# A chunked linear attention and two SwiGLU layers: decay tables turned earlier, state copies and normalising moved to ScalarE, and the last check split

## The chip, the cores and the metric

The kernel runs on one core of a Trainium2 chip. The metric is the time of one execution on the device in microseconds (us), the slowest core's, which here is the only one. Several executions are timed, and their median counts.

## The reference

```python
for t in range(768):                                    # 4 batches, 8 heads, head size 48, all f32
    cur = einsum('bhd,bhe->bhde', u * k[t], v[t])
    y[t] = einsum('bhd,bhde->bhe', r[t], state + cur)
    state = w * state + einsum('bhd,bhe->bhde', k[t], v[t])
x = y as (3072 tokens, 384)
x = (silu(x @ w_gate) * (x @ w_val)) @ w_out            # 384 -> 1536 -> 384
x = x / sqrt(mean(x * x) + 1e-6) * rms_g                # over the 384 of a token
out = (silu(x @ w_gate2) * (x @ w_val2)) @ w_out2
```

## The kernel before

**The attention** is cut into 32 units: 4 batches, 2 halves of the sequence, 4 pairs of heads. A unit scales its keys and queries by tables of powers of the decay `w` (`G` and `F`), computes the products inside a chunk on TensorE (PE), and carries a 128x48 state over the chunks. Batch 0 does this in f32 with chunks of 128; batches 1 to 3 split every operand into two f16 parts and use chunks of 64. `states` (L478 and L644) runs down the chunks on VectorE (DVE), one scalar_tensor_tensor each (`st <- st * w + pd`). A first half ends with a copy of its last state to `carry`, a second half begins with a copy of `carry` (L486, L491, L649, L657); a first half of batches 1 to 3 begins with a copy of the first product out of PSUM (L651).

**The tables** start from the 96 decays. Two DMAs each bring `w` and `u` as 8 rows (`wu_raw`), `turn_tables` (L230) transposes them on PE into PSUM, L235 copies them, and `setup_tables` (L267 to L291) and `setup_g` (L295) compute the powers on DVE in a chain of small instructions. While the loads run, PE multiplies zeros (`warm`, L321): `WARM = (28, 7)` says 28 such matmuls, then 7 before the second unit's output. The keys of each unit arrive in another layout and are transposed on DVE (L383); L391 on DVE and L394 on GpSimd (POOL) scale them, and the first product of the attention is L463.

**The layers** take the 3072 tokens in 8 blocks of 384, and 1536 hidden columns in 12 steps of 128. A step computes a gate and a value product on PE (L820), silu on ScalarE (ACT, L934), two multiplications on DVE (L942, L944), an f16 high part on ACT (L948), its remainder on POOL (L952), and three f16 matmuls per group of 128 tokens into `po` (L830), of which there are three (g = 0, 1, 2). The blocks of both layers are interleaved: (0,0), (0,1), (0,2), (1,0), (0,3), (1,1) and so on, (1,7) last. The weights of both layers come as raw words and are decoded on DVE (L785, L787, L789, L810) and ACT (L769, L774, L806) during the first third of the run.

At the end of a block `evacuate` (L832) scales `po` into `xo`: groups 0 and 2 on DVE, group 1 on ACT. `squares` (L846) sums the squares of `xo` on ACT; after layer 0 `inverse_rms` (L852) computes `ri` on POOL, `normalize` (L866) multiplies the three groups by it on DVE, `turn_x2` (L871) transposes them on DVE, and `store1` and `load_x2` send them over DRAM to layer 1. After layer 1 `store2` writes `out`. `check_range` (L960) then tests all the sums gathered on the way (squares, weight sums, decays in `wok`), adds them up with one PE matmul into `bad`, and every engine reads `bad` and branches to a general path when it isn't 0.

**The order** on every queue is made by a small list scheduler, `Plan` (L71). Each job has an engine, a cost, the jobs it comes after, and hints (`soon`); its rank is the longest path to the end. The job that can start first is taken, among several the one of the highest rank. Each engine then runs its own jobs strictly in that order.

## Time and profile before

| | us |
|---|---|
| median of 3 runs | 1048.23 |
| lowest and highest | 1045.59, 1048.25 |
| the profiled execution, its own time | 1051.98 |
| its span in the profile | 1050.3 |
| busy in it: PE, DVE, ACT, POOL | 978.8, 609.4, 518.7, 456.9 |
| mean granted clock of TensorE | 0.968 |

The times of instructions are those of the profiled execution, counted from the start of its span; 1.7 us of its time lie around the span. Busy shares are means over stages that differ much, so the stages are read apart. The granted clock is in parts of 2.4 GHz. L numbers are lines of the kernel before.

### The profile page before, as it was taken

The numbers are of one execution on the slowest core, as the hardware profiler recorded it, in microseconds if no ns is written. First come the engines' busy times: TensorE is split into PE (matmuls) and PEld (weight loads), VectorE is DVE, ScalarE is ACT, GpSimd is POOL, SyncE is SP. The second block draws the span as 40 slices with busy tenths as digits, with TensorE's granted clock in tenths as the row PEclk, the third lists the DMA queues.
The fourth block names the chain that finished last, engine by engine and source line by source line (L and its number), as shares of the span: only waits on it lengthen the run. The fifth ranks groups of instructions, "written<-read, shape, count | busy, mean of one in ns | idle before, by whom it ended". The sixth has DMA issues, their size and how long they took to land.

```text
span 1050.3 us, 20693 instructions
## 1 busy us (share of the span) xinstructions
PE 978.8 (93%) x8061; PEld 604.7 (58%) x8062; DVE 609.4 (58%) x1120; ACT 518.7 (49%) x1217; POOL 456.9 (43%) x502
## 2 busy tenths in 40 slices
PE   7778798897889999999999999999999999999995
PEld 4645554554555566656666666666666666666663
DVE  6999999999888754546354744645352412231111
ACT  1965566767685743536344643455343523242322
POOL 6257376545455444553355444553444223332221
PEclk8898899998999999999999999999999999999998
DMA  7997155449655421213113321222010100200000
GB/s 181 222 224 190 27 132 150 113 74 183 142 161 70 103 71 27 49 40 92 40 41 63 80 53 37 30 61 69 7 18 8 54 1 1 53 23 1 23 1 27
DMA packets 152699, 77.13 MB, mean 73 GB/s; under 512 B 115472, under 2 KB 141200, under 8 KB 152592
## 3 DMA queue, kind: packets, MB, share of 16 engines
q1 hardware_dynamic: 152208, 75.13, 31.6%
q8 instruction: 65, 1.06, 0.5%
q0 software_dynamic: 384, 0.59, 0.3%
q14 instruction: 42, 0.34, 0.1%
HBM read 66.23 MB, written 9.45 MB: 72 GB/s over the span
## 4 chain that ended last, share of the span: by engine, by line
PE 65%; DVE 13%; DMA 11%; SPq 5%; issue 3%; ACT 2%; POOL 1%; DVEq 0%; ACTq 0%; POOLq 0%
PE pg L820 20%; PE pv L820 20%; PE po L830 20%; DMA raw<-in_moe_w_out_dram 5%; DMA raw<-in_moe_w_gate_dram 3%; DVE fi L787 2%; PE py L611 2%; DVE w L810 2%; SPq L364 2%; DVE fi L789 1%; DMA xs_d<-tt 1%; DVE fi L785 1%; PE pa L622 1%; PE pd L622 1%; DVE st L654 1%
## 5 line engine op out<-in xcount | busy, mean ns | idle before, releaser
L820 PEld LDWEIGHTS <-w 128*128 128x128 f16 x3456 | 337.8, 99 | 246.8 <-issue 35.6
L952 POOL TENSOR_TENSOR hl<-sl,hh 128x384 f16<-128x384 f32 x192 | 186.3, 971 | 432.8 <-ACT hh L948 402.4
L830 PE MATMUL po<-w,hh 128*128 128x384 f16 x1152 | 281.7, 327 | 0.5 <-DVE xo L844 0.5
L948 ACT ACTIVATE hh<-sl 128x384 f16<-128x384 f32 x192 | 100.0, 521 | 342.3 <-DVE sl L942 193.9
L830 PE MATMUL po<-w,hl 128*128 128x384 f16 x576 | 187.9, 326 | 7.2 <-POOL hl L952 7.2
L820 PE MATMUL pg<-xh,w 128*128 128x384 f16 x576 | 164.2, 341 | 15.1 <-DVE sl L944 14.6
L820 PE MATMUL pv<-x2v,w 128*128 128x384 f16 x864 | 157.6, 328 | 2.5 <-ACT sl L934 2.5
L942 DVE SCALAR_TENSOR_TENSOR sl<-sl,pv 128x384 f32<-128x384 f32 x96 | 52.9, 551 | 183.6 <-PE pv L820 175.0
L820 PE MATMUL pv<-xh,w 128*128 128x384 f16 x576 | 158.2, 330 | 0.0
L820 PE MATMUL pg<-x2g,w 128*128 128x384 f16 x864 | 156.1, 326 | 2.1 <-DVE sl L942 1.7
L830 PEld LDWEIGHTS <-hh 128*128 128x128 f16 x1152 | 111.8, 98 | 74.0 <-issue 1.5
L944 DVE TENSOR_TENSOR sl<-sl,pv 128x384 f32<-128x384 f32 x96 | 52.4, 547 | 102.3 <-PE pv L820 102.1
L934 ACT ACTIVATE sl<-pg 128x384 f32<-128x384 f32 x192 | 92.8, 484 | 32.7 <-PE pg L820 30.4
L820 PE MATMUL pg<-xl,w 128*128 128x384 f16 x288 | 98.4, 342 | 0.0
L820 PE MATMUL pv<-xl,w 128*128 128x384 f16 x288 | 95.1, 330 | 0.0
L830 PEld LDWEIGHTS <-hl 128*128 128x128 f16 x576 | 56.4, 98 | 47.8 <-POOL hl L952 11.0
L787 DVE SCALAR_TENSOR_TENSOR fi<-raw,fi 128x384 int32<-128x384 int32 (+1 forms) x48 | 43.6, 915 | 1.1
L810 DVE SCALAR_TENSOR_TENSOR w<-fi,w 128x384 f16<-128x384 f32 (+1 forms) x48 | 42.6, 902 | 0.8 <-ACT w L806 0.6
L654 DVE SCALAR_TENSOR_TENSOR st<-st,p,pd 128x48 f32<-128x48 f32 x120 | 31.8, 265 | 19.3 <-PE pd L622 15.1
L789 DVE SCALAR_TENSOR_TENSOR fi<-raw,fi 128x384 int32<-128x384 int32 (+1 forms) x48 | 40.0, 848 | 0.7
L569 POOL TENSOR_TENSOR ap<-af,ap 128x384 f16<-128x384 f32 x24 | 25.1, 1044 | 33.9 <-ACT ap L566 33.9
L551 DVE STREAM_TRANSPOSE kf<-kts 128x384 f32<-128x384 f32 x24 | 20.8, 865 | 32.4 <-POOL kp L569 32.3
(190 smaller groups left out, 1257.0 us busy)
## 6 DMA issues: line engine op xcount, KB each, us to landing
...
```

The source lines that it names most:

```text
L569: eng.tensor_sub(t[:, 1], x, t[:, 0])
L654: nc.vector.scalar_tensor_tensor(out=st[:, c + 1], in0=st[:, c], scalar=self.w64(), in1=self.pd[:, c], op0=ALU.mult, op1=ALU.add)
L787: vec.scalar_tensor_tensor(out=fis[q], in0=high, scalar=-0x40000000, in1=fis[q], op0=ALU.bitwise_and, op1=ALU.bitwise_or)
L789: vec.scalar_tensor_tensor(out=fis[q], in0=low, scalar=29, in1=fis[q], op0=ALU.logical_shift_right, op1=ALU.bitwise_or)
L810: nc.vector.scalar_tensor_tensor(out=lo, in0=fis.pop(q).bitcast(F32), scalar=2.0**WS, in1=hi, op0=ALU.mult, op1=ALU.subtract)
L820: nc.tensor.matmul(pt, a[:, kt, :], x[:, kt, :], start=i == 0, stop=i == last)
L830: nc.tensor.matmul(po[g], a[:, sl], x, start=f == 0 and i == 0, stop=f == NF - 1 and i == 2)
L934: nc.scalar.activation(out=sl, in_=job[t]["g"], func=AF.Silu, scale=2.0 ** -(WS + (X2S if J[0] else X1S)))
L942: nc.vector.scalar_tensor_tensor(out=sl, in0=sl, scalar=2.0 ** (H2S - WS - V2S), in1=job[t]["v"], op0=ALU.mult, op1=ALU.mult)
L944: nc.vector.tensor_mul(sl, sl, job[t]["v"])
L948: nc.scalar.activation(out=job[t]["h"][0], in_=job[t]["sl"], func=AF.Copy)
L952: nc.gpsimd.tensor_sub(hl, job[t]["sl"], hh)
```

## The change

The 28 warm matmuls become 9 and 14, with `turn` between them, and it no longer waits for the whole of them. The last step of `states` writes straight to `carry`, and the copies that begin a half go from DVE to ACT. `normalize` goes from DVE to ACT. In layer 0 group 0 is evacuated on ACT as well as group 1. In the last block all three groups are evacuated on DVE, and its squares are read out of PSUM by ACT with the same scale; its last remainder `hl` is computed on DVE instead of POOL. The range check without the last block's sums runs before that block's end; the rest of it is a test of 128x3 values and four small matmuls. `wok` is computed after batch 0 rather than with the tables. The costs in the plan of the jobs concerned change with them, so the planner makes a new order.

```diff
 TOK_LO, MAG_MEAN, GAIN_LO = 2.5e-8 ** 2, 1.02, 0.01
+FINITE = 3.0e38
...
-WARM = (28, 7)
+WARM = (9, 14, 7)
...
             else:
-                nc.vector.tensor_copy(st[:, 0], carry[hp])
+                nc.scalar.activation(out=st[:, 0], in_=carry[hp], func=AF.Copy)
             for c in range(self.nd):
+                to = carry[hp] if c == NC - 1 else st[:, c + 1]
                 nc.vector.scalar_tensor_tensor(
-                    out=st[:, c + 1], in0=st[:, c], scalar=w128(hp), in1=self.pd[c], op0=ALU.mult, op1=ALU.add)
-            if self.half == 0:
-                nc.vector.tensor_copy(carry[hp], st[:, NC])
+                    out=to, in0=st[:, c], scalar=w128(hp), in1=self.pd[c], op0=ALU.mult, op1=ALU.add)
...
             if self.half:
-                nc.vector.tensor_copy(st[:, 0], late["carry"][self.hp])
+                nc.scalar.activation(out=st[:, 0], in_=late["carry"][self.hp], func=AF.Copy)
             else:
-                nc.vector.tensor_copy(st[:, 1], self.pd[:, 0])
+                nc.scalar.activation(out=st[:, 1], in_=self.pd[:, 0], func=AF.Copy)
                 c0 = 1
             for c in range(c0, self.nd):
+                to = late["carry"][self.hp] if c == N2 - 1 else st[:, c + 1]
                 nc.vector.scalar_tensor_tensor(
-                    out=st[:, c + 1], in0=st[:, c], scalar=self.w64(), in1=self.pd[:, c], op0=ALU.mult, op1=ALU.add)
-            if not self.half:
-                nc.vector.tensor_copy(late["carry"][self.hp], st[:, N2])
+                    out=to, in0=st[:, c], scalar=self.w64(), in1=self.pd[:, c], op0=ALU.mult, op1=ALU.add)
...
+    def on_act(layer, blk):
+
+        return () if (layer, blk) == (1, NBLK - 1) else (1,) if layer else (0, 1)
+
     def evacuate(layer, blk, g):
...
             scale = 2.0 ** -(X1S + 2 * WS)
-        if g == 1:
+        if g in on_act(layer, blk):
             nc.scalar.activation(out=xo, in_=po, func=AF.Copy, scale=scale)
...
             col = (layer * NBLK + blk) * NG + g
-            nc.scalar.activation(out=sq, in_=post["xo", layer, blk][:, g], func=AF.Square, accum_out=ssall[:, col : col + 1])
+            if (layer, blk) == (1, NBLK - 1):
+                nc.scalar.activation(out=sq, in_=acc[layer, blk][g], func=AF.Square, accum_out=ssall[:, col : col + 1],
+                                     scale=iratio[:, blk * NG + g : blk * NG + g + 1])
+            else:
+                nc.scalar.activation(out=sq, in_=post["xo", layer, blk][:, g], func=AF.Square, accum_out=ssall[:, col : col + 1])
...
         for g in range(NG):
-            nc.vector.tensor_scalar_mul(xo[:, g], xo[:, g], ri[:, 0, g : g + 1])
+            nc.scalar.activation(out=xo[:, g], in_=xo[:, g], func=AF.Copy, scale=ri[:, 0, g : g + 1])
...
         hh, hl = job[t]["h"]
-        nc.gpsimd.tensor_sub(hl, job[t]["sl"], hh)
+        (nc.vector if t == 2 * NT - 1 else nc.gpsimd).tensor_sub(hl, job[t]["sl"], hh)
...
         ns = 3 * (NBLK * HP - NU1)
-        ok = ev.tile([P, n + n // 2 + 3 * NW + ns + 1], F32, tag="sq", name="ok")
+        m = n - NG + n // 2 + 3 * NW + ns + 1
+        ok = ev.tile([P, m], F32, tag="sq", name="ok")
         g2 = ev.tile([P, KT], F32, tag="g2", name="g2")
...
         at = 0
-        for i, bound, op in ((ssall, 3.0e38, ALU.is_le), (ssall[:, : n // 2], TOK_LO * DM, ALU.is_ge),
+        for i, bound, op in ((ssall[:, : n - NG], FINITE, ALU.is_le), (ssall[:, : n // 2], TOK_LO * DM, ALU.is_ge),
                              (wsum[:, :NW], SUM_HI, ALU.is_le), (wsum[:, :NF], MAG_MEAN * 3 * DM, ALU.is_ge),
...
         nc.vector.tensor_reduce(out=m1[:, 1:2], in_=wok, axis=AX.X, op=ALU.min)
-        m2 = ev.tile([P, 1], F32, tag="m2", name="m2")
-        nc.vector.tensor_mul(m2, m1[:, 0:1], m1[:, 1:2])
+        post["m2"] = ev.tile([P, 1], F32, tag="m2", name="m2")
+        nc.vector.tensor_mul(post["m2"], m1[:, 0:1], m1[:, 1:2])
+
+    def check_last():
+
+        ok = ev.tile([P, NG], F32, tag="ok3", name="ok3")
+        nc.vector.tensor_scalar(out=ok, in0=ssall[:, -NG:], scalar1=FINITE, scalar2=None, op0=ALU.is_le)
         pc = ps.tile([P, 1], F32, tag="att0", name="pc")
-        nc.tensor.matmul(pc[0:1], m2, ones, start=True, stop=True)
+        for i in range(NG + 1):
+            nc.tensor.matmul(pc[0:1], ok[:, i - 1 : i] if i else post["m2"], ones, start=i == 0, stop=i == NG)
         bad = ev.tile([1, 1], I32, tag="bad", name="bad")
-        nc.vector.tensor_scalar(out=bad, in0=pc[0:1], scalar1=P - 0.5, scalar2=None, op0=ALU.is_lt)
+        nc.vector.tensor_scalar(out=bad, in0=pc[0:1], scalar1=(NG + 1) * P - 0.5, scalar2=None, op0=ALU.is_lt)
         return bad
...
     add("wu", "D", 1.9, [], load_tables)
-    add("turn", "T", 0.3, ["wu", "c0"], turn_tables)
+    add("turn", "T", 0.3, ["wu", ("warm", 0)], turn_tables)
     add("wraw", "V", 0.1, ["turn"], turned_tables)
...
     add("c1", "G", 1.2, [("v", HP - 1), "table"], setup_consts2)
-    for i, (m, after, soon) in enumerate(zip(WARM, (["c0"], [("d", 0)]), (("tb", 0), ("a", 1)))):
+    for i, (m, after, soon) in enumerate(zip(WARM, (["c0"], ["turn"], [("d", 0)]), ("turn", ("tb", 0), ("a", 1)))):
         add(("warm", i), "T", 0.22 * m + (3.2 if i == 0 else 0), after, lambda m=m: warm(m), soon=[soon])
...
         add(("G", hp), "V", 0.41, ["tables"], lambda hp=hp: setup_g(hp))
-    add("wok", "V", 0.4, ["tables"], decay_range)
+    add("wok", "V", 0.4, ["tables", ("xl", NU1 - 1)], decay_range)
...
         add(("sbd", n), "A", 0.61, [("st", n), "c1"] + prior("y", 2), lambda un=un: un.states2())
-        add(("y", n), "T", 1.95, [("below", n), ("sbd", n), ("f", n)] + prior("xl", back) * first + prior("y", 1) + [("warm", 1)] * (n == 1),
+        add(("y", n), "T", 1.95, [("below", n), ("sbd", n), ("f", n)] + prior("xl", back) * first + prior("y", 1) + [("warm", 2)] * (n == 1),
             lambda un=un, ytag=ytag: un.mm_y(ytag))
...
         add(("hh", t), "A", 0.41, [("m", t)] + prev("o", 2), lambda t=t: step_hh(t))
-        add(("hl", t), "G", 0.95, [("hh", t)], lambda t=t: step_hl(t))
+        add(("hl", t), "V" if t == 2 * NT - 1 else "G", 0.95, [("hh", t)], lambda t=t: step_hl(t))
         if f:
...
         for g in range(NG):
-            add(("e",) + J + (g,), "A" if g == 1 else "V", 0.41 if g == 1 else 0.47, [o] + before, lambda J=J, g=g: evacuate(*J, g))
+            add(("e",) + J + (g,), "A" if g in on_act(*J) else "V", 0.58, [o] + before, lambda J=J, g=g: evacuate(*J, g))
         es = [("e",) + J + (g,) for g in range(NG)]
-        add(("sq",) + J, "A", 1.4, es + [("sq",) + ORD[n_ - 1]] * (n_ > 0), lambda J=J: squares(*J))
+        add(("sq",) + J, "A", 2.1, ([o] if J == ORD[-1] else es) + [("sq",) + ORD[n_ - 1]] * (n_ > 0), lambda J=J: squares(*J))
         if layer == 0:
...
             add(("ri", blk), "G", 2.5, [("sq",) + J] + back("put") + back("sc"), lambda blk=blk: inverse_rms(blk))
-            add(("sc", blk), "V", 1.0, [("ri", blk)], lambda blk=blk: normalize(blk))
+            add(("sc", blk), "A", 1.6, [("ri", blk)], lambda blk=blk: normalize(blk))
             quot = [("vl2", b) for l, b in ORD[: n_ + 2] if l][-1:]
...
                     lambda blk=blk, g=g, n=n: store2(blk, g, g + n))
-    add("check", "V", 1.0, [("sq",) + J for J in ORD] + [("chk",) + q for q in seq] + ["wok", "attended"],
-        lambda: post.__setitem__("bad", check_range()))
+    add("check", "V", 3.0, [("sq",) + J for J in ORD[:-1]] + [("chk",) + q for q in seq] + ["wok", "attended", "rmsg"],
+        check_range)
+    add("bad", "V", 0.5, ["check", ("sq",) + ORD[-1]] + [("e",) + ORD[-1] + (g,) for g in range(NG)],
+        lambda: post.__setitem__("bad", check_last()))
...
         plan.run()
```

The first place is DVE at the start, from the zeroing of `uw` on. `first` holds the keys and queries of a unit, `wu` the turned decays. Before, the two transposes of the first unit stood ahead of the tables:

```order
L917 MEMSET uw 128x8
L383 STREAM_TRANSPOSE first_174<-first_174 128x12x32 [waits DMAHW6_49,DMAHW7_49,DMAHW5_49,DMAHW4_49]
L383 STREAM_TRANSPOSE first_174<-first_174 128x12x32 [waits DMAHW2_49,DMAHW3_49,DMAHW1_49,DMAHW0_49]
L235 COPY wu<-pw 128x8 [waits PE_49]
L270 TENSOR_SCALAR pw<-wu 128x4 [waits DVE_49]
L273 TENSOR_TENSOR pw<-pw 128x4 [waits DVE_49]
```

Now they stand behind nearly all of the tables (the second block begins with their last instruction but two):

```order
L292 TENSOR_SCALAR iE<-iE,zm 128x64 [waits DVE_49,Pool_49]
L384 STREAM_TRANSPOSE first_155<-first_155 128x12x32 [waits DMAHW2_49,DMAHW3_49,DMAHW1_49,DMAHW0_49]
L296 TENSOR_TENSOR G<-iE,ipw 128x128 [waits DVE_49]
L296 TENSOR_TENSOR F<-E,pw 128x128
L384 STREAM_TRANSPOSE first_155<-first_155 128x12x32 [waits DMAHW6_49,DMAHW7_49,DMAHW5_49,DMAHW4_49]
L392 TENSOR_TENSOR first_155<-first_155,G 128x384 [waits DVE_49]
L320 TENSOR_TENSOR uw<-wu,pw 64x4 x2
L384 STREAM_TRANSPOSE first_166<-first_166 128x12x32 [waits DMAHW6_49,DMAHW7_49,DMAHW5_49,DMAHW4_49]
```

The two L384 rows moved from ahead of the chain of small instructions into it.

The second place is ACT in the middle, where block (0,1) is normalised and the first second half of batch 1 starts. `w` is a decoded weight, `hh` and `sl` belong to a layer's step, `x2g` is a loaded block of layer 1, `sb` the scaled states that the unit's matmuls use. Before:

```order
L806 ACTIVATE w_2_2860<-fi_3049 128x384 [waits DVE_49]
L774 ACTIVATE mag,wsum<-mag,mlo 128x384 [waits Activation_49]
L806 ACTIVATE w_2_2860<-fi_3090 128x384 [waits DVE_49]
L934 ACTIVATE sl<-pg 128x384 [waits PE_49]
L906 ACTIVATE x2g<-xt,gains 128x384 [waits DMAHW6_49,DMAHW7_49,DMAHW5_49,DMAHW0_49]
L906 ACTIVATE x2g<-xt,gains 128x384 x2
L665 ACTIVATE sb<-st,p_100 64x6x48 [waits DVE_49]
L665 ACTIVATE sb<-st,p_100 64x6x48
```

Now three multiplications by `ri`, of which the first waits for POOL, and the copy of `carry` stand there, ahead of `hh` and `sl` of a step and of `sb`:

```order
L805 ACTIVATE w_2_2849<-fi_3006 128x384 [waits DVE_49]
L773 ACTIVATE mag,wsum<-mag,mlo 128x384 [waits Activation_49]
L805 ACTIVATE w_2_2849<-fi_3027 128x384 [waits DVE_49]
L876 ACTIVATE xo<-xo,ri 128x384 [waits Pool_49]
L876 ACTIVATE xo<-xo,ri 128x384 x2
L649 ACTIVATE st<-carry_1313 128x48
L955 ACTIVATE hh<-sl 128x384 [waits DVE_49]
L941 ACTIVATE sl<-pg 128x384 [waits PE_49]
L664 ACTIVATE sb<-st,p_100 64x6x48 [waits DVE_49,Activation_49]
L664 ACTIVATE sb<-st,p_100 64x6x48
```

Behind each of the waiting rows stand those of other chains, which start only after it.

The third place is the end of the program, on DVE first. Before, the last evacuation is followed by the whole check, which ends so:

```order
L975 TENSOR_SCALAR ok<-sqs 128x72
L975 TENSOR_SCALAR ok<-gs 128x1 [waits DVE_49]
L979 TENSOR_REDUCE m_13225<-ok 128x1 [waits DVE_49]
L980 TENSOR_REDUCE m_13225<-wok 128x1
L982 TENSOR_TENSOR m_13228<-m_13225 128x1 [waits DVE_49]
L986 TENSOR_SCALAR bad<-pc 1x1 [waits PE_49]
```

Now:

```order
L949 SCALAR_TENSOR_TENSOR sl<-sl,pv 128x384 [waits PE_49,Activation_49,Pool_49] x10
L959 TENSOR_TENSOR hl<-sl,hh 128x384 [waits Activation_49]
L847 TENSOR_SCALAR xo<-po_12804,iratio 128x384 [waits DMAHW6_49,PE_49]
L847 TENSOR_SCALAR xo<-po_12805,iratio 128x384 [waits Activation_49]
L847 TENSOR_SCALAR xo<-po_12806,iratio 128x384 [waits Activation_49]
L995 TENSOR_SCALAR ok_13209<-ssall 128x3
L1000 TENSOR_SCALAR bad<-pc 1x1 [waits PE_49]
```

The reductions moved ahead of the last block's end, `hl` and three evacuations stand where two did, and the second and third of these wait for ACT. On ACT the end is now:

```order
L955 ACTIVATE hh<-sl 128x384 [waits DVE_49,Pool_49]
L941 ACTIVATE sl<-pg 128x384 [waits PE_49]
L955 ACTIVATE hh<-sl 128x384 [waits DVE_49,Pool_49]
L854 ACTIVATE sq,ssall<-po_12804,iratio 128x384 [waits DVE_49]
L854 ACTIVATE sq,ssall<-po_12805,iratio 128x384 [waits PE_49,Activation_49]
L854 ACTIVATE sq,ssall<-po_12806,iratio 128x384 [waits PE_49,Activation_49]
```

The squares read `po` instead of `xo`; the first waits for DVE's evacuation of the same tile, the others for PE and for the square ahead of them.

## Rows read from the trace of the kernel before

**Rows 1.** Stretches: span, busy us of PE, PEld, DVE, ACT, POOL; clock, DMA share, GB/s.

```profile
30.00:130.00 100.00, 78.81 (x515) 52.93 (x516) 95.43 (x120) 67.58 (x117) 51.58 (x39) 0.88 0.69 163
130.00:330.00 200.00, 170.84 (x1587) 103.29 (x1587) 190.22 (x356) 142.47 (x386) 109.11 (x118) 0.94 0.59 133
...
400.00:1000.00 600.00, 599.06 (x4999) 368.75 (x4998) 251.46 (x485) 252.22 (x578) 238.20 (x268) 1.00 0.17 38
```

**Rows 2.** Waits of PE, 130 to 330 us: total us, times, longest us.

```profile
PE pg L820 <- DVE sl L944: 7.6, 5, 3.2
PE py L611 <- DVE sb L667: 7.5, 4, 4.1
...
PE pv L820 <- ACT sl L934: 2.5, 1, 2.5
...
PE py L611 <- ACT ap L566: 2.3, 2, 1.3
PE pg L820 <- DVE sl L942: 1.7, 1, 1.7
```

**Rows 3.** Timeline of the start: start us, us, engine, line, operation, count, [idle before].

```profile
4.78 0.15 PEld L325 LDWEIGHTS <-zeros 128*128 128x128 bf16 x1 [0.27 <-issue]
...
6.96 0.86 DVE L383 STREAM_TRANSPOSE first<-first 128x384 f32<-128x384 f32 x1 [5.35 <-DMA first<-in_k_dram]
...
9.24 0.87 DVE L383 STREAM_TRANSPOSE first<-first 128x384 f32<-128x384 f32 x1 [1.43 <-DMA first<-in_r_dram]
...
10.23 0.22 PE L232 MATMUL pw<-ident,wu_raw 8*128 8x8 f32 x1
10.49 0.17 DVE L235 COPY wu<-pw 128x8 f32<-128x8 f32 x1 [0.38 <-PE pw L232]
...
14.84 1.24 POOL L394 TENSOR_TENSOR first<-first,F 128x384 f32<-128x384 f32 x1 [4.83 <-DVE F L295]
```

**Rows 4.** Groups of lines on DVE, 20 to 130 us.

```profile
L486 DVE COPY st<-carry 128x48 f32<-128x48 f32 x4 | 2.2, 546 | 0.0
...
L491 DVE COPY carry<-st 128x48 f32<-128x48 f32 x4 | 1.4, 354 | 0.1
```

**Rows 5.** The same on DVE, 130 to 330 us.

```profile
L869 DVE TENSOR_SCALAR xo<-xo,ri 128x384 f32<-128x384 f32 x9 | 4.4, 544 | 0.0
...
L844 DVE TENSOR_SCALAR xo<-po 128x384 f32<-128x384 f32 x6 | 3.0, 548 | 0.0
...
L657 DVE COPY carry<-st 128x48 f32<-128x48 f32 x4 | 2.3, 569 | 0.1
...
L651 DVE COPY st<-pd 128x48 f32<-128x48 f32 x4 | 0.8, 194 | 0.0
L649 DVE COPY st<-carry 128x48 f32<-128x48 f32 x3 | 0.5, 175 | 0.0
```

**Rows 6.** Groups of lines on ACT over the whole span.

```profile
L496 ACT ACTIVATE sbd<-st,p 64x144 f32<-64x144 f32 x16 | 6.5, 408 | 4.1 <-DVE st L488 4.0
L842 ACT ACTIVATE xo<-po,iratio 128x384 f32<-128x384 f32 x8 | 4.6, 580 | 5.3 <-PE po L830 5.3
```

**Rows 7.** Timeline of a block's end in the PE-bound part.

```profile
432.36 1.11 DVE L869 TENSOR_SCALAR xo<-xo,ri 128x384 f32<-128x384 f32 x3 [3.15 <-POOL ri L859]
...
434.02 0.52 ACT L948 ACTIVATE hh<-sl 128x384 f16<-128x384 f32 x1 [3.52 <-DVE sl L942]
```

**Rows 8.** Timeline of the end of the program.

```profile
1037.47 0.91 POOL L952 TENSOR_TENSOR hl<-sl,hh 128x384 f16<-128x384 f32 x1 [3.47 <-ACT hh L948]
...
1038.81 0.62 DVE L844 TENSOR_SCALAR xo<-po,iratio 128x384 f32<-128x384 f32 x1 [2.03 <-PE po L830]
...
1040.41 0.52 ACT L850 ACTIVATE sq<-xo 128x384 f32<-128x384 f32 x1
...
1041.06 0.52 ACT L850 ACTIVATE sq<-xo 128x384 f32<-128x384 f32 x1
...
1043.51 0.15 DVE L986 TENSOR_SCALAR bad<-pc 1x1 int32<-1x1 f32 x1 [0.28 <-PE pc L984]
```

## The prediction

> **What bounds the kernel now.** I read the table of stretches first [rows 1]. From 400 to 1000 us PE is busy for 599.06 of 600 us at a granted clock of 1.00: there PE is the bound, and work taken off another engine gives nothing. From 30 to 130 us DVE is busy 95.43 of 100, and from 130 to 330 us 190.22 of 200, while PE has 170.84 of 200: PE sits idle for 29.2 us in the second of these stretches, and DVE hardly at all. So the first third is paced mostly by DVE, which decodes the weights there. The change can gain in three places only: the time before DVE is full (the start), the first third, and the end, where one chain runs alone.
>
> Next the waits of PE in the second stretch [rows 2]. Three of them end on a DVE instruction, 7.6 + 7.5 + 1.7 = 16.8 us, and two on an ACT instruction, 2.5 + 2.3 = 4.8 us. Of PE's 29.2 idle us, 0.58 are thus DVE's and 0.16 ACT's; the rest is mainly POOL's. The reader should see that taking 1 us from DVE need not give 1 us, and that ACT, busy 142.47 of 200 [rows 1], isn't free either.
>
> Then the timelines of the start [rows 3] and the end [rows 8], where single instructions count.
>
> **The change part by part.** The sum is made against the profiled execution's 1051.98 us, 3.75 above the median of 1048.23; I carry the difference to the median.
>
> *Turn and tables.* The turn is at 10.23, its copy at 10.49, and POOL's scaling of the first queries, which ends the chain of tables, at 14.84 [rows 3]: 4.35 us from copy to scaling. Now nine matmuls stand ahead of the turn, and the tenth load of zeros was at 4.78. Its other input, the DMA of `w` and `u`, isn't shown by a wait; on its queue it was issued ahead of the first keys, which DVE got at 6.96 after waiting for them. So the turn comes between 4.8 and 7.0; I take 5.3, near the lower end, since the keys come in four pieces behind it. The copy is then at 5.56. But the two transposes of the first unit, 0.86 and 0.87 us, which lay in DVE's idle time, now stand inside the chain: 5.56 + 4.35 + 1.73 = 11.6 instead of 14.84. Gain 3.2 us; with the turn at 4.8 it is 3.7, at 7.0 it is 1.5. The queries land before 9.24, so they don't hold it. Five fewer warm matmuls cost nothing where PE only waits. Behind the tables DVE is nearly full (95.43 of 100 from 30 us on), so the shift lasts unless loads hold it. `wok` leaves the start and comes back after batch 0 on the same full engine: two instructions on four columns, 0.2 us each by the copy at 10.49, taken as zero in sum.
>
> *Carry written directly.* 4 copies of L491 leave DVE, 1.4 us [rows 4], and 4 of L657 before 330 us, 2.3 us [rows 5]. No engine gets them. The 8 later ones lie where PE is the bound: zero.
>
> *State copies to ACT.* 4 of L486 (2.2 us), 4 of L651 (0.8) and 3 of L649 (0.5) leave DVE by 330 us [rows 4, 5]. What a 128x48 copy costs on ACT no row shows. The nearest are 408 ns for 64x144 with a pointer as scale [rows 6] and, with eight times the columns, 520 ns for 128x384 [rows 7]; below, zero. I take 0.3 us, under the 0.41, and 0 and 0.5 as ends.
>
> *Normalising on ACT.* 9 multiplications by 330 us leave DVE, 4.4 us [rows 5], and come to ACT at 0.58 each, by the evacuation with a pointer as scale [rows 6]: 5.2 us. The other 15 lie where PE is the bound. There they have cover: DVE normalised at 432.36, after a wait of 3.15 us for POOL, and ACT idled 3.52 us until `hh` at 434.02 [rows 7]; three times 0.58 from 432.4 end at 434.1. If that cover is gone, `hh` of a step comes later by at most that.
>
> The row says 0.49 us per multiplication on DVE (4.4 / 9) against 0.58 on ACT, so the move costs more than it frees and pays only because DVE is the fuller. The Trainium skill, "ScalarE: Activation LUTs", section "Rules for kernel authors", says for a `mul`: use VectorE, not ScalarE. By that rule the 4.4 us would stay on DVE, 5.2 us would not come to ACT, and the forecast's middle would be smaller by 1.7 us (0.58 x 4.4 - 0.16 x 5.2).
>
> *Evacuation of group 0.* By 330 us 3 of the 6 evacuations of L844 leave DVE, 1.5 us [rows 5], for 3 x 0.58 = 1.7 us of ACT.
>
> *The middle's sum.* From DVE, 130 to 330 us: 4.4 + 1.5 + 2.3 + 0.8 + 0.5 = 9.5 us. To ACT: 5.2 + 1.7 + 7 x 0.3 = 9.0 us. By the shares above, 9.5 x 0.58 - 9.0 x 0.16 = 5.5 - 1.4 = 4.1 us. From 20 to 130 us I count only L491, which nobody gets: 1.4 x 0.58 = 0.8; for L486 nothing, since ACT, which gets it, also makes the `sbd` that follows it. What is late next, where a wait for DVE goes, is a decoded weight or POOL's `ap`.
>
> *The end.* `hl` took POOL 0.91 us from 1037.47 [rows 8]; on DVE I take the 0.62 of the evacuation (bounds 0.4 and 0.91), so the first evacuation moves from 1038.81 to 1038.5 and ends at 1039.1. The squares begin only then, since the first waits for this evacuation on DVE. They ran 0.65 us apart (1040.41, 1041.06), so the third runs from 1040.4 to 1041.0. The third evacuation waits for it: to 1041.7. The 128x3 test (0.15 by the `bad` row), then matmuls (0.28 idle before `bad`; three more, at most 0.22 each by the turn's row, taken as 0.05), put `bad` at about 1042.3 instead of 1043.51. Gain 1.2 us; if the two engines read side by side, the last 0.62 and one square fall out too: 2.5. The lower bound is 0.8, if each handoff costs 0.1 more. Stores lie beside it.
>
> Sum: 3.2 + 0.8 + 4.1 + 1.2 = 9.3 us. The profiled execution would be 1042.7, and the median 1048.23 - 9.3 = **1038.9 us**.
>
> **The rivals.**
>
> *The middle gives nothing.* PE's waits in the first third go from DVE to POOL, ACT or a DMA. For it: DMA share 0.59 [rows 1], and a quarter of PE's idle time is neither DVE's nor ACT's. Against it: 16.8 us are DVE's. Start and end alone give 4.4: 1043.8.
>
> *All of DVE's time converts.* DVE is busy 190 of 200, so each us taken off could shorten the stretch. 3.2 + 1.4 + 9.5 + 1.2 = 15.3: 1032.9; with the end's upper bound 1031.6. Against it: ACT gets 9.0 us, and PE's waits name others too.
>
> *Slower: ACT's queue becomes the gate.* ACT runs in order, and `normalize` stands ahead of `hh`, `sl` and `sb`, waiting for POOL's `ri`. Where DVE waited 3.15 us for it [rows 7], everything behind it on ACT waits as long: 3 blocks by 330 us, 9.5 us. Eleven state copies each come behind one 0.52 us instruction of ACT and add their own 0.3: 9.0 us. If all of it reached PE, 18.5 lost and 9.3 gained make 1057.4. It decides from 12.4 us lost (then slower by over 0.3%). Against it: DVE was in order too and had no such waits before 330 us (idle 0.0 before L869 [rows 5]), since it came late. The skill's rule above, for VectorE, points this way.
>
> *The start is held.* The first weights' loads keep to their queue whatever the tables do (DMA share 0.69 from 30 to 130 [rows 1]), or ACT can't follow. Then 0.8 + 4.1 + 1.2 = 6.1: 1042.1.
>
> *It doesn't do what it says.* The turn still comes late for its loads, the middle absorbs the rest, and the evacuations and squares wait for each other so that nothing lies beside anything: the end's 0.8 alone, 1047.4.
>
> **How the numbers follow.** Chances: the forecast (1036 to 1041.5) 0.42; the middle nothing 0.19; all converts 0.12; slower 0.09; the start held 0.10; nothing of it 0.08. About 0.3%, 3.1 us, is what a measurement of this kernel can tell from no change. Under 1045.1 lie the forecast and three rivals, 0.83, less 0.07 for those near 1043 that spill over: faster 0.76. The same: 0.15. Slower: 0.09. The range goes from 1031.6, all converting with the end's upper bound, to 1047.4, the end alone. It leaves out the slower rival and half of the last one, with little below: under 0.2.
>
> **What would show it.** The turn near 5.3 and POOL's first scaling near 11.6; DVE under 190 of 200 in the stretch that was 130 to 330, PE's waits for L944 and L667 smaller; `bad` some 1.2 us nearer to the last `hh`. Wrong would be: PE's idle time of 29.2 us unchanged and put down to ACT (`sl`, `ap`, `sb`) or POOL; the copy of the state on ACT long after `pd`; raw weights decoded at the same times as before though the tables are earlier; or PE no longer full after 400 us.

## The result, and the profile after

Beside six runs of the kernel before with a median of 1048.51 us, the changed kernel's six have a median of **1038.72 us** (1035.08 to 1042.33). The ratio is 0.9899, with a 95% interval from 0.9871 to 0.9926. The forecast was 1038.9 us, in a range from 1031.6 to 1047.4. In later executions of both the ratio was 0.9878 (0.9848 to 0.9908).

The two profiled executions stand further apart than the medians: 1051.98 us before, 1035.08 after, the fastest of its six. So 7 of the 16.9 us between them belong to these two executions, and below a second profile of the changed kernel (1042.54 us, the slowest of its six) is read beside the first. Of the lines after, L819 is what L820 was, L847 is L844, L876 is L869, L949 and L951 are L942 and L944.

The stretches after, which answer to [rows 1]: span, busy us of PE, PEld, DVE, ACT, POOL; clock, DMA share, GB/s.

```profile
30.00:130.00 100.00, 76.72 (x503) 50.66 (x503) 93.85 (x130) 64.77 (x113) 56.50 (x43) 0.91 0.68 162
130.00:330.00 200.00, 175.70 (x1635) 107.58 (x1633) 183.01 (x324) 151.31 (x409) 113.25 (x120) 0.96 0.60 137
...
400.00:1000.00 600.00, 600.00 (x4922) 369.05 (x4920) 233.13 (x449) 263.39 (x609) 234.27 (x265) 1.00 0.16 38
```

From 130 to 330 us DVE is busy 183.01 instead of 190.22, ACT 151.31 instead of 142.47 (the 9.0 us put on it), and PE 175.70 instead of 170.84, so that its idle time there falls by 4.9 us. From 400 us on PE is full, as before. The waits of PE from 130 to 330 us, beside [rows 2] (total us, times, longest us):

```profile
PE pg L819 <- DVE sl L951: 5.2, 3, 2.5
PE py L611 <- DVE sb L666: 3.9, 2, 2.9
PE py L611 <- ACT ap L566: 3.8, 2, 2.7
PE py L611 <- POOL ap L569: 3.7, 4, 1.9
PE pg L819 <- DVE sl L949: 3.0, 1, 3.0
```

The waits for DVE fell from 16.8 to 12.1 us, those for `sb` from 7.5 to 3.9. ACT's are 3.8 for `ap`, where 2.3 were; with 1.2 for `sl` and 0.9 for `xo` they make 5.9, where 4.8 were.

The start, beside [rows 3]:

```profile
5.34 0.27 PE L233 MATMUL pw<-ident,wu_raw 8*128 8x8 f32 x1
...
9.34 0.85 DVE L384 STREAM_TRANSPOSE first<-first 128x384 f32<-128x384 f32 x1
...
10.68 1.00 POOL L395 TENSOR_TENSOR first<-first,F 128x384 f32<-128x384 f32 x1 [0.67 <-DVE F L296]
...
12.23 1.42 PE L464 MATMUL att<-first 64*128 64x128 f32 x12 [3.13 <-DVE first L392]
```

The turn is at 5.34 (taken: 5.3), POOL's first scaling at 10.68 (taken: 11.6) instead of 14.84. Only one of the two transposes lies in the chain ahead of it: POOL scales what was transposed first. PE's first product starts at 12.23 instead of 16.13.

The end, beside [rows 8]:

```profile
1021.49 0.56 DVE L959 TENSOR_TENSOR hl<-sl,hh 128x384 f16<-128x384 f32 x1 [0.65 <-ACT hh L955]
...
1022.48 0.62 DVE L847 TENSOR_SCALAR xo<-po,iratio 128x384 f32<-128x384 f32 x1 [0.43 <-PE po L829]
...
1024.54 0.58 ACT L854 ACTIVATE sq<-po,iratio 128x384 f32<-128x384 f32 x1
1024.54 1.32 DVE L847 TENSOR_SCALAR xo<-po,iratio 128x384 f32<-128x384 f32 x2 [1.44 <-ACT sq L854]
...
1026.32 0.15 DVE L1000 TENSOR_SCALAR bad<-pc 1x1 int32<-1x1 f32 x1 [0.38 <-PE pc L998]
```

From the start of the last `hl` to the end of `bad` it was 6.19 us (1037.47 to 1043.66) and is 4.98. DVE's second evacuation waits 1.44 us for ACT's second square; it then runs beside the third square, and the third evacuation behind that.

How far the changed kernel is ahead can be followed along the 192 f16 high parts `hh`, one per step. The table gives the start of some of them in the profile of the kernel before, and in other profiles the difference from it, in us:

| profile | 1st | 9th | 25th | 33rd | 73rd | 192nd |
|---|---|---|---|---|---|---|
| before, at | 62.03 | 130.94 | 226.14 | 283.95 | 483.95 | 1036.87 |
| changed kernel, first profile | -6.11 | -6.97 | -7.91 | -13.75 | -15.63 | -15.93 |
| changed kernel, second profile | -0.52 | -2.70 | -3.65 | -7.22 | -8.08 | -8.38 |
| start alone | -1.91 | -2.08 | -1.46 | +1.13 | +2.47 | +2.46 |
| start alone, more warm matmuls | -4.81 | -5.28 | -4.64 | -2.00 | -0.30 | -0.19 |
| late turn | -1.30 | -2.54 | -4.73 | -10.12 | -11.98 | -12.29 |
| without the start part | -0.11 | -1.38 | -1.66 | -5.40 | -7.66 | -8.06 |
| the moves to ACT undone | -4.10 | -4.79 | -4.01 | -10.00 | -10.06 | -6.47 |
| normalising on DVE | -5.38 | -6.33 | -4.99 | -10.16 | -10.50 | -10.81 |
| copies that begin a half on DVE | -0.54 | -1.02 | -2.12 | -9.64 | -12.06 | -12.36 |
| carry copies back | -0.34 | -1.26 | -1.45 | -7.31 | -8.11 | -7.93 |

Two things are to be seen. One and the same kernel starts 6.1 or 0.5 us ahead. And from the 25th to the 33rd step, a stretch of 58 us, it gains 5.8 or 3.6 us at once; the granted clock there is 0.97 in the first profile and 0.91 in the second and in the kernel before. A difference of some 2 us between two single profiles therefore says little by itself.

### The profile page after: what moved, and what is told of

It reads as the page before. It is cut to its first block, busy times and chain, and to the rows that moved or that the text cites. A ratio compares the mean times of both kernels' runs of the same rounds, so it can differ in the third digit from the quotient of the medians.

```text
span 1033.3 us, 20690 instructions
## 1 busy us (share of the span) xinstructions
PE 970.5 (94%) x8063; PEld 601.5 (58%) x8063; DVE 579.2 (56%) x1047; ACT 538.7 (52%) x1276; POOL 459.4 (44%) x501
## 4 chain that ended last, share of the span: by engine, by line
PE 68%; DMA 10%; DVE 9%; SPq 5%; ACT 4%; issue 3%; POOL 0%; DVEq 0%; ACTq 0%; POOLq 0%
PE pg L819 22%; PE pv L819 21%; PE po L829 21%; DMA raw<-in_moe_w_gate_dram 3%; DMA raw<-in_moe_w_out_dram 3%; PE py L611 2%; SPq L365 2%; DVE fi L786 2%; DMA raw<-in_moe_w_val_dram 1%; DVE fi L788 1%; PE pa L622 1%; PE pd L622 1%; DVE fi L784 1%; DVE st L655 1%; DVE w L809 1%
## 5 line engine op out<-in xcount | busy, mean ns | idle before, releaser
L819 PEld LDWEIGHTS <-w 128*128 128x128 f16 x3456 | 336.3, 99 | 244.1 <-issue 30.7
L819 PE MATMUL pg<-xh,w 128*128 128x384 f16 x576 | 162.7, 338 | 15.1 <-DVE sl L951 15.0
L949 DVE SCALAR_TENSOR_TENSOR sl<-sl,pv 128x384 f32<-128x384 f32 x96 | 53.1, 553 | 204.8 <-PE pv L819 180.9
L819 PE MATMUL pg<-x2g,w 128*128 128x384 f16 x864 | 157.2, 328 | 3.8 <-DVE sl L949 3.0
L819 PE MATMUL pv<-x2v,w 128*128 128x384 f16 x864 | 156.9, 327 | 1.2 <-ACT sl L941 1.2
L819 PE MATMUL pv<-xh,w 128*128 128x384 f16 x576 | 156.3, 326 | 0.0
L951 DVE TENSOR_TENSOR sl<-sl,pv 128x384 f32<-128x384 f32 x96 | 52.6, 549 | 101.7 <-PE pv L819 101.0
L819 PE MATMUL pg<-xl,w 128*128 128x384 f16 x288 | 97.5, 339 | 0.0
L819 PE MATMUL pv<-xl,w 128*128 128x384 f16 x288 | 93.9, 326 | 0.0
L655 DVE SCALAR_TENSOR_TENSOR st<-st,p,pd 128x48 f32<-128x48 f32 x108 | 28.5, 264 | 46.7 <-ACT st L651 20.9
L809 DVE SCALAR_TENSOR_TENSOR w<-fi,w 128x384 f16<-128x384 f32 (+1 forms) x48 | 40.3, 860 | 1.8 <-ACT w L805 1.8
L768 ACT ACTIVATE mag<-raw 128x384 bf16<-128x384 f32 (+1 forms) x48 | 34.8, 726 | 11.5 <-DMA raw<-in_moe_w_out_dram 8.7
L805 ACT ACTIVATE w<-fi 128x384 f16<-128x384 f32 (+1 forms) x48 | 31.8, 677 | 13.6 <-DVE fi L788 13.5
```

Source lines behind the costliest of these rows:

```text
L655: nc.vector.scalar_tensor_tensor(out=to, in0=st[:, c], scalar=self.w64(), in1=self.pd[:, c], op0=ALU.mult, op1=ALU.add)
L768: nc.scalar.activation(out=mags[q], in_=word_views(raws[q])[1].bitcast(F32), func=AF.Abs, accum_out=wsum[:, w_col(q) : w_col(q) + 1])
L809: nc.vector.scalar_tensor_tensor(out=lo, in0=fis.pop(q).bitcast(F32), scalar=2.0**WS, in1=hi, op0=ALU.mult, op1=ALU.subtract)
L819: nc.tensor.matmul(pt, a[:, kt, :], x[:, kt, :], start=i == 0, stop=i == last)
L949: nc.vector.scalar_tensor_tensor(out=sl, in0=sl, scalar=2.0 ** (H2S - WS - V2S), in1=job[t]["v"], op0=ALU.mult, op1=ALU.mult)
L951: nc.vector.tensor_mul(sl, sl, job[t]["v"])
```

## The experiments

**The start alone, and all but the start.** The first kernel is that of before with the turn amid the warm matmuls and `wok` behind batch 0; the second is the changed kernel without these.

```diff
-WARM = (28, 7)
+WARM = (9, 14, 7)
...
-    add("turn", "T", 0.3, ["wu", "c0"], turn_tables)
+    add("turn", "T", 0.3, ["wu", ("warm", 0)], turn_tables)
...
-    add("wok", "V", 0.4, ["tables"], decay_range)
+    add("wok", "V", 0.4, ["tables", ("xl", NU1 - 1)], decay_range)
```

> The kernel before with the start of the change alone: 9, 14 and 7 warm matmuls with the turn between the first two groups, and the decay test after batch 0. My theory (the tables come 3 to 4 us earlier, DVE is full behind them, so the shift lasts): turn near 5.3, POOL's first scaling near 10.7 instead of 14.84, the first f16 high part of a step 3 to 5 us earlier, 1043.5 to 1045.5 us in all. Rival 'the start is held' (loads or ACT take the shift back by the first third): turn just as early, but first high part less than 1 us earlier, and 1047.5 to 1049. Second rival (the start is worth all that shows at the first high part of the changed kernel, 6.1 us): 1042.4.

Measured: 1051.63 us (12 runs) beside 1051.31 for before, ratio 1.0001 (0.9984 to 1.0017). The turn was as early as in the changed kernel (5.33), but the first `hh` only 1.91 us ahead, and all of it was gone by the 33rd.

> The changed kernel with the start of the kernel before (28 and 7 warm matmuls, turn behind the 28, decay test with the tables). My theory: 3 to 4.5 us of the gain go, 1042 to 1043.5, turn at 10.2. Rival 'the start is held': no loss, 1038 to 1039.5. Second rival (6.1 us): 1044.8.

Measured: 1043.91 us beside the same 1051.31, ratio 0.993 (0.991 to 0.995): 7.4 us are gained without the start part. Between this and the changed kernel's 0.9878 to 0.9899 lie 3.3 to 5.5 us. The start is worth nothing by itself and several us in the whole. Both kernels, however, have an order of their own, since the planner starts from other times; so the next ones keep the order of every queue.

**The changed kernel again, and with a late turn.** The first is the changed kernel as it is.

> The changed kernel once more, to stand beside the next three on one chip. Between 0.986 and 0.991 of the kernel before. In one profile of it the first f16 high part of a step came 6.1 us earlier than before, in the kernel with the later squares, whose start is the same, 0.5 us earlier, with the granted clock at 0.50 for longer between 12 and 28 us. If the clock of the start is what spreads the runs, this profile falls at one of these two, and its time with it: near the lower or the upper end of the runs.

Measured: 1038.58 us (1035.41 to 1042.54), ratio 0.9878 (0.9848 to 0.9908). Its profile, of 1042.54 us, is the second one in the table: with its first `hh` only 0.52 us ahead it fell at the upper end, as the text on the clock expected. The second kernel has the warm matmuls divided as 22 and 1 (the plan still counts 9 and 14):

```diff
-        add(("warm", i), "T", 0.22 * m + (3.2 if i == 0 else 0), after, lambda m=m: warm(m), soon=[soon])
+        add(("warm", i), "T", 0.22 * m + (3.2 if i == 0 else 0), after, lambda m=m, i=i: warm((22, 1, 7)[i]), soon=[soon])
```

> The changed kernel, every queue in the same order, but 22 warm matmuls ahead of the turn and 1 behind it instead of 9 and 14: the turn comes near 9.2 us. My theory (the early turn itself is worth 3 to 5 us): 3 to 5 us slower than the changed kernel of the same call. Rival (the loss of 5 us without the start part came from the other order that the planner made, and loads or the clock eat the shift): within 1.5 us of it.

Measured: 1044.58 us, ratio 0.9933 (0.991 to 0.9955), 6.0 us slower than the 1038.58 of the changed kernel beside it. The turn on PE was at 9.10:

```profile
9.10 0.22 PE L233 MATMUL pw<-ident,wu_raw 8*128 8x8 f32 x1
```

By the two ratios of the changed kernel the early turn is worth 3.6 to 5.8 us with an unchanged order, 6.0 by the medians: the loss without the start part didn't need another order. Part of it goes with the clock, however. Seven of the nine executions with the late turn have mean clocks of 0.967 to 0.969 and took 1044.4 us in the mean; the three of the changed kernel's twelve at 0.968 to 0.970 took 1041.9. The other two, at 0.976 and 0.977, took 1039.0; the changed kernel's four at 0.975 to 0.977 took 1035.7. So between executions of like clocks the early turn is worth 2.5 to 3.3 us, and the rest is that low clocks came more often with the late turn. Whether the late turn brings them about, nine executions don't show.

**More warm matmuls.** The granted clock from 12 to 28 us differs between the two profiles of one kernel. First the kernel before, then the changed kernel's first and second profile (columns as above, the clock third from the end):

```profile
12.00:20.00 8.00, 3.87 (x21) 3.65 (x21) 7.64 (x22) 0.00 (x0) 4.20 (x4) 0.61 0.72 182
20.00:28.00 8.00, 6.95 (x59) 5.09 (x60) 7.52 (x15) 4.91 (x15) 4.95 (x5) 0.75 1.03 240
```

```profile
12.00:20.00 8.00, 7.18 (x41) 4.96 (x42) 7.67 (x16) 2.36 (x7) 5.52 (x6) 0.57 0.62 170
20.00:28.00 8.00, 8.00 (x83) 7.67 (x82) 7.40 (x15) 6.87 (x20) 5.05 (x5) 1.00 1.07 263
```

```profile
12.00:20.00 8.00, 6.92 (x38) 5.28 (x40) 7.29 (x14) 2.36 (x7) 5.02 (x6) 0.53 0.62 161
20.00:28.00 8.00, 8.00 (x47) 7.31 (x46) 4.96 (x13) 4.01 (x11) 3.89 (x4) 0.50 1.06 257
```

PE ran at 1.2 GHz, 0.50, in parts of these stretches. In the first profile it was back at 1.00 by 20 us, in the second it stayed at 0.50 until 28. To keep PE at work for longer, 28 warm matmuls were put behind the turn instead of 14, in the order of the changed kernel:

```diff
+        ... lambda m=m, i=i: warm((9, 28, 7)[i]), soon=[soon])
```

> The changed kernel, every queue in the same order, but 28 warm matmuls behind the turn instead of 14, so that PE works on until about 12 us, where the first product waits for it. Theory 'the clock of the start' (PE idles from 9.1 to 12.2, and the granted clock falls to 0.50 for the f32 products that follow): granted clock 1.00 up to 16 us or later, first high part 5 to 6 us earlier than before in every run, runs spread by less than 3 us instead of 7, median 1 to 3 us under the changed kernel's. Rival (the clock falls for what comes after, the thin f32 work): clock 0.50 in 13 to 20 us again, same spread, median within 1 us.

Measured: 1038.79 us (1036.8 to 1044.89), ratio 0.9895 (0.9861 to 0.9928), no better. The first `hh` was 3.12 us ahead instead of the 5 to 6 expected, and the spread was 8.1 us, where less than 3 was expected.

```profile
12.00:20.00 8.00, 7.02 (x62) 5.33 (x61) 7.54 (x15) 2.36 (x7) 5.37 (x6) 1.00 0.65 172
20.00:28.00 8.00, 6.22 (x41) 6.11 (x42) 5.84 (x14) 4.70 (x13) 3.74 (x5) 0.57 1.03 248
```

The fall came later: 1.00 from 12 to 20, 0.57 from 20 to 28, behind 2.06 us in which PE waited for ACT. So that wait was filled with 9 more (and the squares of the last block come later, see below):

```diff
+        lambda un=un, tags=tags, n=n: (un.mm_a(tags), warm(9) if n == 1 else None)
```

> The changed kernel with the later squares of the last block, 28 warm matmuls behind the turn, and 9 more between the second unit's scores and the matmuls that wait for ScalarE there (PE idle 2.06 us in the run with more warm matmuls, and the clock at 0.50 behind it). Theory 'the clock of the start follows PE's gaps': granted clock 1.00 from 9 to 27 us, first high part 5 us or more earlier than before, every run near the lower end of the changed kernel's, ratio 0.984 to 0.987, spread under 4 us. Rival (the thin f32 work itself lets the clock fall, wherever the gaps are): a dip to 0.50 again between 20 and 36 us, ratio 0.987 to 0.990, the same spread.

Measured: 1037.52 us (1036.35 to 1040.06), ratio 0.9894 (0.9879 to 0.991).

```profile
12.00:20.00 8.00, 7.00 (x53) 5.27 (x56) 7.60 (x16) 2.36 (x7) 5.47 (x6) 0.79 0.63 164
20.00:28.00 8.00, 8.00 (x75) 6.43 (x74) 6.69 (x15) 6.21 (x18) 4.50 (x5) 1.00 0.92 230
```

The clock is 0.79 and 1.00 in the two stretches, and the mean clock of its five runs 0.977 (the changed kernel's runs have 0.968 to 0.977). The first `hh` was 4.75 us ahead, nearly the 5 expected; the better ratio didn't come. The spread is 3.7 us, where the changed kernel had 7.1. That the matmuls narrowed it isn't shown: five runs of the kernel with the later squares alone spread by 4.4 us, and five with normalising on DVE (below), which has no more warm matmuls than the changed kernel, by 2.0. Then the same extra matmuls with the start alone:

> The kernel with the start of the change alone, every queue in its order, with the same extra warm matmuls (28 and 9). The start alone gave 1.0001. Theory 'the clock took the start's gain back' (its runs had a mean clock of 0.967 against 0.971): with the clock held the ratio falls to 0.996 to 0.998. Rival 'the order of the queues behind the start, or the loads, took it': 0.999 to 1.001 though the clock between 12 and 27 us is higher.

Measured: 1049.87 us beside 1049.26, ratio 0.9999 (0.9985 to 1.0013).

```profile
12.00:20.00 8.00, 7.08 (x52) 5.24 (x54) 7.71 (x15) 2.36 (x7) 5.68 (x6) 0.79 0.63 167
20.00:28.00 8.00, 8.00 (x75) 6.44 (x74) 7.12 (x16) 6.17 (x17) 4.89 (x5) 1.00 1.04 243
```

The clock was up, the first `hh` 4.81 us ahead, and still nothing was left at the end: that the clock took the start's gain back falls. From the 9th to the 73rd step 5.0 us went. The largest piece is one wait of PE for DVE's `sl` at L944, 7.27 us, longer than any wait of PE behind 130 us in the kernel before (4.1):

```profile
251.91 0.48 PE L820 MATMUL pg<-xh,w 128*128 128x384 f16 x1 [7.27 <-DVE sl L944]
```

DVE had no idle time there. Its timeline shows what stood ahead of that `sl`:

```profile
243.21 0.96 DVE L785 TENSOR_SCALAR fi<-raw 128x384 int32<-128x384 int32 x1
...
248.99 0.55 DVE L810 SCALAR_TENSOR_TENSOR w<-fi,w 128x384 f16<-128x384 f32 x1
249.46 1.49 DVE L876 STREAM_TRANSPOSE tt<-xo 128x384 f32<-128x384 f32 x3
250.88 0.51 DVE L810 SCALAR_TENSOR_TENSOR w<-fi,w 128x384 f16<-128x384 f32 x1
251.31 0.54 DVE L944 TENSOR_TENSOR sl<-sl,pv 128x384 f32<-128x384 f32 x1
```

Two raw weight tiles are decoded (six instructions with those left out), a block is transposed and two weights are finished, and only then comes the `sl` that PE needs. The run with the start alone had the same wait, 7.42 us. But the kernel before has a long wait at the same place, for `sb` behind the decoding:

```profile
251.16 0.24 PE L611 MATMUL py<-rp,sb 128*128 128x64 f16 x1 [4.12 <-DVE sb L667]
```

From 226 to 284 us PE waits for DVE 12.3 us in all here and 8.5 in the kernel before, and from the 25th to the 73rd step, where 4.3 of the 5.0 us go, 15.7 and 10.6. The planner's order places `sb` ahead of the decoding here and behind it in the kernel before, and DVE has the same work ahead of what PE needs either way. From 130 to 330 us DVE itself waits a little more for loads: 3.0 us for raw weights (2.0 before) and 0.9 for queries (none listed before). So the largest part of the loss lies where PE waits for DVE. That it is lost at that one place isn't shown, and how much of it the order made and how much the loads wasn't tested; in the changed kernel's order the longest wait for an `sl` behind 130 us is 3.0 us.

**The moves to ACT.** First all three undone in the changed kernel, at the places of its order:

```diff
-            nc.scalar.activation(out=xo[:, g], in_=xo[:, g], func=AF.Copy, scale=ri[:, 0, g : g + 1])
+            nc.vector.tensor_scalar_mul(xo[:, g], xo[:, g], ri[:, 0, g : g + 1])
...
-                nc.scalar.activation(out=st[:, 0], in_=late["carry"][self.hp], func=AF.Copy)
+                nc.vector.tensor_copy(st[:, 0], late["carry"][self.hp])
...
-        if g in on_act(layer, blk):
+        if g == 1 and on_act(layer, blk):
```

> The changed kernel with the normalising, the copies that begin a half and the evacuation of group 0 of layer 0 on DVE again, all at the places that the changed kernel's order gives them; carry is still written directly. My theory (DVE's time counts by 0.58 and ACT's by 0.16 in the first third): 7.2 us back on DVE and 9.0 off ACT before 330 us make 1041 to 1042.5. Rival 'all of DVE's time converts': 1045 to 1046. Rival 'ACT's queue is the gate': faster than the changed kernel, 1036 or less. Rival 'the middle gives nothing': 1038 to 1039.5.

Measured: 1045.09 us beside 1051.31, ratio 0.9952 (0.9928 to 0.9976), 5.6 to 7.8 us slower than the changed kernel. More than I had: but the table shows that 3.6 us of it are lost behind the 73rd step, where I had put zero. PE waits there once in every second block (some 116 us apart), 0.8 us each; from 500 us on:

```profile
PE po L829 <- POOL hl L959: 3.2, 4, 0.8
```

The kernels with one of the moves undone lose nothing there (the rows for the normalising and for the copies that begin a half), so it goes with the evacuation of group 0 on DVE in this order, or with the three together; that wasn't taken apart. What is striking is the stretch from the 25th to the 33rd step: with all three moves undone, and only the copies to carry left out, it still gains 6.0 us.

Then the normalising alone:

> The changed kernel, every queue in its order, with the 24 normalising multiplications on DVE again. My theory (4.4 us of DVE by 330 us at 0.58, less 5.2 of ACT at 0.16): 1.7 us slower than the changed kernel, ratio 0.990 to 0.992. 'DVE converts whole, ACT costs nothing' (the run with all three moves undone lost 6 us of 7.2): 4.0 slower, 0.992 to 0.994. The rule that a multiplication belongs on DVE: faster than the changed kernel, 0.987 or less.

Measured: 1042.25 us beside 1049.26, ratio 0.993 (0.9916 to 0.9943), 3.3 to 5.5 us slower than the changed kernel. The waits of PE from 130 to 330 us:

```profile
PE pg L819 <- DVE sl L951: 5.4, 4, 2.4
PE py L611 <- ACT ap L566: 5.2, 2, 4.2
...
PE pg L819 <- DVE sl L949: 4.0, 1, 4.0
```

Each is longer than in the changed kernel (5.2, 3.8 and 3.0), and PE is busy for 171.68 of these 200 us instead of 175.70. On DVE the nine multiplications took more than the 4.4 us that they took in the kernel before:

```profile
L876 DVE TENSOR_SCALAR xo<-xo,ri 128x384 f32<-128x384 f32 x9 | 5.5, 662 | 0.1
```

So 3.3 to 5.5 us were lost for 5.5 us put on DVE and 4.9 taken off ACT; by the shares of 0.58 and 0.16 it would be 2.4. The loss is nearer to the whole than to the share, but the intervals are wide (0.9916 to 0.9943, and 0.9871 to 0.9926 or 0.9848 to 0.9908 for the changed kernel). And the multiplication that costs 0.61 us on ACT is well placed there:

```profile
L876 ACT ACTIVATE xo<-xo,ri 128x384 f32<-128x384 f32 x9 | 4.9, 606 | 0.5 <-POOL ri L866 0.5
...
L845 ACT ACTIVATE xo<-po 128x384 f32<-128x384 f32 x6 | 2.6, 484 | 0.0
...
L651 ACT ACTIVATE st<-pd 128x48 f32<-128x48 f32 x4 | 0.8, 188 | 0.0
...
L649 ACT ACTIVATE st<-carry 128x48 f32<-128x48 f32 x3 | 0.7, 228 | 0.0
```

The Trainium skill, "ScalarE: Activation LUTs", section "Rules for kernel authors", would keep a `mul` on VectorE; here the measurement decides against it: the kernel is slower with them on DVE, the fuller engine (183.01 of 200 us busy, ACT 151.31).

The copies that begin a half alone:

> The changed kernel, every queue in its order, with the copies that begin a half on DVE again (28 of them, 11 by 330 us). My theory (1.3 us of DVE behind 130 us at 0.58, nothing for the four before): 0.4 us slower than the changed kernel, ratio 0.988 to 0.990. 'DVE converts whole' (1.3 + 2.2): 3.5 slower, 0.991 to 0.993. 'ACT's queue is late with these copies' (DVE waited 3.7 us for L649 and 1.0 for L651 in the changed kernel): faster by 1 to 4 us, 0.984 to 0.987.

Measured: 1038.15 us beside 1049.26, ratio 0.9877 (0.9857 to 0.9897). Moving them to ACT gains nothing that can be seen. A copy costs little on ACT, 0.19 to 0.23 us, where I took 0.3. But the changed kernel's DVE waits for them, from 20 to 330 us (total us, times, longest us):

```profile
DVE st L490 <- ACT st L487: 4.3, 3, 2.7
DVE st L655 <- ACT st L649: 3.7, 3, 1.4
...
DVE st L655 <- ACT st L651: 1.0, 1, 1.0
```

Together 9.0 us in which DVE waits, against the 3.5 us that the eleven copies took on DVE ([rows 4, 5]: 2.2, 0.8, 0.5). In part DVE would have waited there anyway, for the products that the copy or the next step reads. With the copies on DVE again it does:

```profile
DVE st L490 <- PE po L471: 2.3, 1, 2.3
...
DVE st L490 <- PE att L471: 1.8, 1, 1.8
```

That is 4.1 us. In these two profiles the handoff thus adds 4.9 us of waiting, more than the 3.5 us that the copies freed.

**The copies to carry**, back in the changed kernel:

```diff
+            if self.half == 0:
+                nc.vector.tensor_copy(carry[hp], st[:, NC])
...
+            if not self.half:
+                nc.vector.tensor_copy(late["carry"][self.hp], st[:, N2])
```

> The changed kernel, every queue in the same order, with the 16 copies of the last state to carry on DVE again. My theory: 1.4 us of DVE by 130 us and 2.3 by 330 us, counted by 0.58, make it 1.3 to 2.2 us slower. Rival 'all converts': 3.7. Rival 'nothing': within 0.5.

Measured: 1042.69 us beside the changed kernel's 1038.58, ratio 0.9922 (0.9894 to 0.9951): 4.1 us slower. That looks like all of the 3.7 us that DVE spent on the eight copies by 330 us in the kernel before, but here they took 1.6, by groups of lines on DVE from 20 to 330 us:

```profile
L658 DVE COPY carry<-st 128x48 f32<-128x48 f32 x4 | 0.8, 189 | 0.1
L492 DVE COPY carry<-st 128x48 f32<-128x48 f32 x4 | 0.8, 188 | 0.1
```

PE's waits for `sl` from 130 to 330 us:

```profile
PE pg L821 <- DVE sl L953: 7.8, 4, 2.7
```

They were 5.2 us, and PE is idle for 26.3 of these 200 us, where it was idle for 24.3 and 22.6 in the two profiles of the changed kernel. In the table, though, this run is level with the second profile from the 33rd step on, at a clock of 0.97 from 130 to 330 us where that one had 0.94. So the copies cost something; that they cost their own time and no more isn't shown, and neither is why the loss is larger than 1.6 us.

**The end.** The squares of the last block are written behind all three evacuations, so that an evacuation no longer waits for a square:

```diff
-        add(("sq",) + J, "A", 2.1, ([o] if J == ORD[-1] else es) + [("sq",) + ORD[n_ - 1]] * (n_ > 0), lambda J=J: squares(*J))
+        add(("sq",) + J, "A", 2.1, es + [("sq",) + ORD[n_ - 1]] * (n_ > 0), lambda J=J: squares(*J))
```

> The changed kernel with the last block's squares written after its three evacuations instead of ahead of the second, so that no evacuation waits for a square, and each square waits for the evacuation of its own tile. Theory (in the changed kernel DVE's second and third evacuation stand behind ACT's squares, 1.44 us idle): the stretch from the start of the last hl to the end of bad shrinks from 4.98 us to about 4.4, the total by the same 0.5, which the times won't show (1038.2). Rival (the two engines also slow each other down where they read the same memory at once): the stretch stays at 4.9 to 5.0, with longer evacuations or squares than 0.62 and 0.58.

Measured: 1038.37 us, ratio 0.986 (0.9838 to 0.9882).

```profile
1026.91 0.56 DVE L959 TENSOR_TENSOR hl<-sl,hh 128x384 f16<-128x384 f32 x1 [0.65 <-ACT hh L955]
...
1027.90 1.67 DVE L847 TENSOR_SCALAR xo<-po,iratio 128x384 f32<-128x384 f32 x3 [0.43 <-PE po L829]
...
1029.96 0.58 ACT L854 ACTIVATE sq<-po,iratio 128x384 f32<-128x384 f32 x1
...
1031.22 0.15 DVE L1000 TENSOR_SCALAR bad<-pc 1x1 int32<-1x1 f32 x1 [0.38 <-PE pc L998]
```

From the start of `hl` to the end of `bad` it is 4.46 us instead of 4.98, and evacuations and squares keep 0.62 and 0.58 us though they run side by side on different tiles. The chain shows the 0.5 us, the times don't separate this kernel from the changed one. It is the best that was run, by what its profile shows.

## Why the prediction was right, and where it wasn't

**The total** was right: 9.3 us forecast, 9.8 measured (and 12.6 in the later executions, beside 1051.18). That the terms may be added up was not: the start is worth nothing alone and several us in the whole.

**The end**, 1.2 us: right, 6.19 to 4.98. `hl` on DVE took 0.56 (0.62 taken), and the serial chain of evacuation, squares and test came as worked out.

**The start**, 3.2 us: the chain of tables was right (5.34 for 5.3) and a little pessimistic behind it. The step "Behind the tables DVE is nearly full (95.43 of 100 from 30 us on), so the shift lasts unless loads hold it" failed for the start alone. It gives nothing (1.0001), and the clock doesn't explain that (0.9999 with the clock up): PE loses the shift from the 25th to the 73rd step, where it waits for DVE; what the order and the loads have in it stays open. With the rest of the change the early turn gives 3.6 to 6.0 us, and 2.5 to 3.3 between executions of like clocks, which is what was forecast. And it is not one number: the first `hh` came 6.1 or 0.5 us ahead in two executions of one kernel, with the clock's return at 20 or at 28 us.

**The middle**, 4.1 and 0.8 us: about right or too small. From the 9th to the 73rd step the two profiles gain 8.7 and 5.4 us, beside a kernel before whose profiled execution was itself 3.5 us above its median. All but the start gives 7.4 us with 1.2 of it at the end; 6.2 for 4.9, and the interval (0.991 to 0.995) leaves 4.1 to 8.3, so 4.9 isn't excluded. PE's idle time from 130 to 330 us fell by 4.9 us. The weak step is the share of 0.58, taken from whom PE's waits name: what was undone cost more than its share (normalising 3.3 to 5.5 us for 1.7, all three moves 5.6 to 7.8 for 2.7, the copies to carry 4.1 for 2.1, the last within the interval). That DVE's time came back whole isn't shown: on DVE again the multiplications took 5.5 us and not 4.4, the copies to carry 1.6 and not 3.7. So the rows of the kernel before, from which the sum took DVE's times, weren't fixed prices either. ACT's instructions cost about what was taken (0.61 for 0.58, 0.48 for 0.58, 0.2 for 0.3).

**The state copies**, 0.4 us by the shares: nothing that can be seen, and 0.4 us couldn't be. What the sum left out is the handoff: DVE waits for ACT's copy before its first step down the chunks, 4.9 us more than it waits for PE without it.

**The rivals.** "All of DVE's time converts" was nearer when normalising and the copies to carry were undone, but for the whole change its 15.3 us lie beyond the 9.8 and 12.6 measured. "ACT's queue becomes the gate" is there only as the 9.0 us that DVE waits for copies; `normalize` waited 0.5 us for POOL by 330 us, not 9.5, since it comes late in ACT's queue as it did in DVE's. "The middle gives nothing" and "the start is held" fall for the whole change, the second holds for the start alone, and whether by the loads that it named stays open.

**What stays open.** From the 25th to the 33rd step every kernel with the changed order gained between 3.4 and 7.5 us, whichever part was undone; the kernel before has there its longest wait for `sb`, 4.1 us [rows 2]. This points to a part of the middle's gain that belongs to the order that the new costs made, and not to the time freed. It isn't shown: each of these kernels still had part of the time freed, and the old instructions in the new order, which would tell, weren't run. The single losses (3.6 to 6.0 for the start, 3.3 to 5.5 for normalising, 4.1 for carry, and 1.2 at the end) add up to about as much as the change gains or more; with intervals of 1.4 us and more on each side they don't tell whether the parts are independent. That the start gives nothing alone does: they aren't.
